# Early copies of two block products, later output products in batch 0, and weight combinations from four raw blocks

## The chip, the cores and the metric

One core of a Trainium2 chip runs the program. The metric is the time of one execution on the device, in microseconds (us); lower is better. The core has five engines with queues of their own: TensorE (PE; its weight loads are listed as PEld), VectorE (DVE), ScalarE (ACT), GpSimd (POOL), and SyncE (SP), whose queue issues the DMAs here.

## The reference

Three layers run one after the other over x of 4 batches, 1088 positions and 128 features, all in float32. The first is an attention with products of linear features, the second a gated channel mix, and the third, where the change lies, a gMLP block:

```python
h = np.maximum(x @ w_in, 0.0)                     # 128 -> 1024
u, v = h[..., :512], h[..., 512:]
v_n = (v - mu) / np.sqrt(var + 1e-06)             # over the 512 features
v_s = np.einsum('ts,bsd->btd', w_spatial, v_n) + b_spatial[None, :, None]
return ((u * v_s) @ w_out).astype(np.float32)     # 512 -> 128
```

w_spatial is 1088 x 1088: one matrix mixes the positions of every batch and feature.

## The kernel before

Matrices are held as a high part H (rounded to the matmul's 32-bit format) and a low part L = x - H. The helper `mm3` (line 124) multiplies such a pair by another in three matmuls. `copy` (line 127) makes H on ACT; `low` (line 130) makes L on DVE or POOL.

Attention and channel mix run up to about 206 us. The rest is the spatial product, in two ways.

**Batch 0** multiplies directly. A unit (function `spatial`) is one block d of 128 features by one chunk c of positions (384, 384 and 320 columns); `ORD0` lists the 12 units, four of which run earlier. A unit makes u (`pre` part, relu on ACT at line 519), sums eight position tiles k = 0..7 and a tail into `acc`, multiplies on DVE (line 529) and hands the result to `put_out`: H on ACT, L on DVE, and a closure in the list `gout`. A later unit pops that closure behind its own tile k == 3; it multiplies by w_out into a bank of PSUM. Between the tiles a unit also starts other work from the table `fill`: the tiles v of batch 1 (`v_tile`), and the combinations of weight blocks for the batches to come (`W2`).

**Batches 1 to 3** cut the positions 0..767 against 0..767 in blocks of two by two and use a scheme with seven block products in place of eight. It needs combinations of the four 384-wide raw blocks W11, W12, W21, W22 for each k of 0..3: part 1 = W12 - W11, part 3 = W22 - W12, part 2 = W22 - W12 + W11, part 4 = W21 - part 2. Part 4 takes the place of W12 in SBUF, which batch 0 reads for chunk 1. `first_load` and `first_sums` ("fl", "fs") read raw blocks by DMA (line 574) into slots of `VR`, make sums on DVE (`tt`, line 577) and split them (`parts`: ACT, then POOL). `second_load` and `second_sums` ("sl", "ss") do the rest. The slots 3 to 8 of `VR` serve these loads and later `quad_load` (line 632), which fetches blocks of the normalised v back from DRAM for `build`, which combines and splits them.

A **group** (function `group`) is one batch and a pair of feature blocks d, e = p, p + 2; there are six. Its products go to three banks: X (bank 0), Y (bank 1) and Z (bank 6). Each product (`prod`) is 12 matmuls; `tmm` (lines 675 and 676) adds the tail. Products 2 and 3 add to X, 4 adds to Z. `snap` copies a bank to SBUF on ACT, `join` adds a bank and such a copy on DVE (line 577), `gated_out` multiplies by relu of `pre` (line 689) and calls `put_out`. The end of a group before the change is

```python
prod(X, 3, 3, False); tmm(X, e, wtile(NK, 1))
u3 = snap(X)
gated_out(pre(e, 1), join(Z, u3, c22), e, 1)      # Z holds product 1
gated_out(pre(e, 0), join(Y, u3), e, 0)           # Y holds product 22 x 4
prod(Z, 4, 22, False)                             # adds to Z: after the join has read it
```

so the product 4 may not start before the join has read Z, and the next group's first product, which starts bank X afresh, not before `snap` has read X.

The program is written down as a list, and a planner, which uses a model of the engines' times, then orders the instructions of each engine: what it takes for ready goes ahead, earlier lines of the program first among ready ones. So a place in the program is a rank and no fixed slot; once planned, each engine runs its queue strictly in that order.

Of the kernel before, what the change touches and what calls it, by code (L numbers as in the profile page):

```python
# [19 lines left out]
DG = 512  # L20
# [41 lines left out]
W2 = {4: ((6, "fl", 2),), 5: ((1, "fs", 2), (1, "fl", 3)), 6: ((1, "fs", 3), (2, "fl", 0)),  # L62
      7: ((1, "fs", 0), (2, "fl", 1)), 8: ((1, "fs", 1), (4, "sl", 2), (4, "sl", 0)), 9: ((1, "ss", 2), (4, "ss", 0), (7, "sl", 1)),
      10: ((4, "ss", 1), (7, "sl", 3)), 11: ((4, "ss", 3),)}
FSET = ((3, 4, 5), (6, 7, 8))
SSET = {2: (7, 8), 0: (5, 6), 1: (7, 8), 3: (7, 8)}
# [12 lines left out]
def attn_moe_gmlp(ctx: ExitStack, tc: tile.TileContext, qT, kT, va, st, wk, wv, wr, win, wout,  # L79
# [325 lines left out]
    wt, xsp, vnt, tl, vdram = {}, {}, {}, {}, {}  # L405
# [50 lines left out]
    def v_tile(b, j, banks=(6, 7)):  # L456
        xH, xL = xsp[b]
        v = VR[:, j] if b == 0 else VR[:, rot(-1, -2, -3) + 3] if j < NK else vtail[:, 0]
        pv = bank(rot(*banks))
        cs = slice(128 * j, 128 * j + 128)  # L460
        mm3(pv, xH[:, cs], xL[:, cs], winH[:, DG:], winL[:, DG:], True, True, 0)
        SE.activation(out=v, in_=pv, func=AF.Relu)  # L462
        bn = sb(rot("bn0", "bn1"), [128, 6])
        mv = sb(rot("mv0", "mv1"), [128, 2])
        rs = sb(rot("rs0", "rs1"), [128, 1])
        VE.bn_stats(out=bn, in_=v)  # L466
        VE.bn_aggr(out=mv, in_=bn)
        GE.tensor_scalar(out=rs, in0=mv[:, 1:2], scalar1=1e-6, scalar2=None, op0=ALU.add)
        GE.tensor_tensor(out=rs, in0=rs, in1=half, op=ALU.pow)  # L469
        VE.tensor_scalar(out=v, in0=v, scalar1=mv[:, 0:1], scalar2=rs, op0=ALU.subtract, op1=ALU.mult)  # L470
        if b and j < NK:
            if j == 0:
                vdram[b] = dr.tile([128, NK, DG], F32, tag=f"vd{b}", bufs=1, name=f"vd{b}")
            nc.sync.dma_start(out=vdram[b][:, j], in_=v)
# [32 lines left out]
    def spatial(b, d, c, fill, early=False):  # L507
# [13 lines left out]
        for k in range(NK):  # L521
            mm3(acc, Hs[k], Ls[k], *wtile(k, c), k == 0, False, 0)
            if k == 3 and gout:
                gout.pop(0)()
            for fn in fill.get(k, ()):
                fn()
# [57 lines left out]
    def first_load(k):  # L584
        raws[k] = [stage(j) for j in rot(*FSET)]
        for x, n in zip(raws[k], (11, 12, 22)):
            wraw(x, n, k)
# [6 lines left out]
    def first_sums(k):  # L594
        r11, r12, r22 = raws.pop(k)
        tt(VE, r11, r12, r11, ALU.subtract)
        parts(1, k, r11)
        tt(VE, r22, r22, r12, ALU.subtract)
        parts(3, k, r22)

    def second_load(k):
        raws[k] = [stage(j) for j in SSET[k]]
        for x, n in zip(raws[k], (11, 21)):
            wraw(x, n, k)

    def second_sums(k):
        a, c = raws.pop(k)
        H, L = [x.bitcast(F32) for x in ctile(3, k)]
        tt(VE, a, a, H, ALU.add)
        tt(VE, a, a, L, ALU.add)  # L610
        tt(VE, c, c, a, ALU.subtract)
        parts(2, k, a)
        parts(4, k, c)
# [34 lines left out]
    def group(b, p):  # L648
# [50 lines left out]
        a = snap(X)  # L699
# [10 lines left out]
        gated_out(pu, join(Y, a), d, 0)  # L710
# [7 lines left out]
        tmm(Y, e, ctile(5, NK))  # L718
        flush()
# [12 lines left out]
        flush()  # L732
        yield
        Z = bank(6)[:, :CMAX]
        prod(Z, 1, 1, True)
        yield
        prod(X, 3, 3, False)
        tmm(X, e, wtile(NK, 1))
        u3 = snap(X)
        pu = pre(e, 1)  # L740
        c22 = sb(rot(m(8), m(9), m(10), m(11)), [128, CMAX])
        gated_out(pu, join(Z, u3, c22), e, 1)
        pu = pre(e, 0)
        gated_out(pu, join(Y, u3), e, 0)
        yield
        prod(Z, 4, 22, False)
        tmm(Z, d, wtile(NK, 1))
        if last_group:
            while gout:
                flush()  # L750
            pu = pre(d, 1)
# [207 lines left out]
    xsplit(1)  # L959
    for u, (d, c) in enumerate(ORD0):  # L960
        if u < EARLY:
            continue
        fill = {}

        def add(k, fn, *a):
            fill.setdefault(k, []).append(lambda: fn(*a))

        for k in range(WB[u] if u < len(WB) else 0):
            add(k, wstep)
        for n, j in enumerate({4: (0, 1), 5: (2, 3), 6: (4, 5), 7: (6, 7)}.get(u, ())):  # L970
            add(2 + 3 * n, v_tile, 1, j)
        for k, fn, *a in W2.get(u, ()):
            add(k, {"fl": first_load, "fs": first_sums, "sl": second_load, "ss": second_sums}[fn], *a)
        if u == 9:
            for n in (11, 12):
                add(2, quad_load, 1, 0, n)
        if u == 11:
            for n in (22, 21):
                add(0, quad_load, 1, 0, n)
        if u == 10:  # L980
            add(2, tails, 1, 0, vtail[:, 0])
            add(1, build, 1, 0, 0)
        if u == 11:
            add(1, build, 1, 0, 1)
        spatial(0, d, c, fill)
    assert wi[0] >= len(worder) and not pending_raw
    groups = [(b, p) for b in range(1, B) for p in range(2)]
    for gi, (b, p) in enumerate(groups):
        nxt = groups[gi + 1] if gi + 1 < len(groups) else None
        if gi == 0:  # L990
            tail_sums()
            build(1, 0, 2)
            tails(1, 2, vtail[:, 0])
            build(1, 0, 3)
        if p == 0 and b + 1 < B:
            xsplit(b + 1)
        for st, _ in enumerate(group(b, p)):
# [4 lines left out]
            if nxt:  # L1002
# [4 lines left out]
                if st in (5, 6):  # L1007
                    tails(nxt[0], nxt[1] + 2 * (st - 5), vtail[:, 0])
# [63 lines left out]
```

## Time and profile before

| | us |
|---|---|
| median of three runs | 472.14 (471.73 to 472.79) |
| profiled execution, whole | 474.71 |
| profiled execution, first to last instruction (span) | 472.9 |

The profile is of one execution. A stretch "206:271" counts from the start of the span. For PE the trace knows starts; a matmul's end is modelled, so in a dense row of matmuls each starts before the one ahead of it is shown as ended, and idle time is counted from the modelled end. PE is busy in 95% of the span, DVE in 61%, ACT in 55%, POOL in 52%.

### The profile page before, as it was taken

The numbers are of one execution on the slowest core, as the hardware profiler recorded it, in microseconds if no ns is written. First come the engines' busy times: TensorE is split into PE (matmuls) and PEld (weight loads), VectorE is DVE, ScalarE is ACT, GpSimd is POOL, SyncE is SP. The second block draws the span as 40 slices with busy tenths as digits, with TensorE's granted clock in tenths as the row PEclk, the third lists the DMA queues.
The fourth block names the chain that finished last, engine by engine and source line by source line (L and its number), as shares of the span: only waits on it lengthen the run. The fifth ranks groups of instructions, "written<-read, shape, count | busy, mean of one in ns | idle before, by whom it ended". The sixth has DMA issues, their size and how long they took to land.

```text
span 472.9 us, 7556 instructions
## 1 busy us (share of the span) xinstructions
PE 447.5 (95%) x2685; PEld 421.6 (89%) x2685; DVE 288.1 (61%) x501; ACT 260.6 (55%) x600; POOL 244.7 (52%) x287
## 2 busy tenths in 40 slices
PE   8978999999999998998988999999999999999995
PEld 8967998989998887998877999899899899999995
DVE  4598767767546795347785784772575751623513
ACT  2485878888776976784443644343535433433322
POOL 2566546486444988368645644445434534333320
PEclk9999999999999999999998999999999999999999
DMA  6973100011000120145454311313022222010001
GB/s 212 362 238 91 49 0 2 17 35 53 24 1 1 52 62 6 33 119 154 138 182 149 115 60 50 109 44 113 14 79 83 74 91 81 18 39 24 0 1 47
DMA packets 31525, 35.70 MB, mean 75 GB/s; under 512 B 2880, under 2 KB 27008, under 8 KB 31488
## 3 DMA queue, kind: packets, MB, share of 16 engines
q1 hardware_dynamic: 31488, 35.22, 23.3%
q8 instruction: 21, 0.34, 0.3%
q14 instruction: 16, 0.13, 0.1%
HBM read 26.69 MB, written 8.52 MB: 74 GB/s over the span
## 4 chain that ended last, share of the span: by engine, by line
PE 59%; DVE 16%; POOL 10%; DMA 5%; issue 4%; ACT 4%; SPq 1%; POOLq 0%; ACTq 0%; DVEq 0%
PE p L124 47%; DVE VR L470 4%; PE p L398 4%; DVE w L130 2%; DMA VR<-in_wT_dram 2%; POOL m L355 2%; PE p L270 2%; DVE bn L466 2%; POOL rs L469 2%; PE p L232 2%; DMA w<-in_wk_dram 2%; DVE w L140 1%; POOL w L130 1%; PE p L201 1%; DMA w<-in_qT_dram 1%
## 5 line engine op out<-in xcount | busy, mean ns | idle before, releaser
L124 PE MATMUL p<-m,k 128*128 128x384 f32 (+1 forms) x288 | 65.8, 348 | 2.7 <-POOL k L145 1.6
L124 PE MATMUL p<-w,k 128*128 128x384 f32 (+1 forms) x360 | 64.1, 324 | 2.4 <-DVE m L577 2.4
L355 POOL TENSOR_TENSOR m<-m 128x384 f32<-128x384 f32 (+1 forms) x48 | 42.8, 897 | 39.2 <-ACT m L352 33.6
L124 PEld LDWEIGHTS p<-w,k 128*128 128x128 f32 x360 | 59.1, 188 | 3.9 <-DVE m L577 3.3
L130 POOL TENSOR_TENSOR k<-VR,k 128x512 fp32r<-128x512 f32 x26 | 33.9, 1305 | 47.4 <-ACT k L127 35.4
L577 DVE TENSOR_TENSOR m<-p,m 128x384 f32<-128x384 f32 (+2 forms) x37 | 19.2, 520 | 61.0 <-PE p L676 34.1
L124 PEld LDWEIGHTS p<-m,k 128*128 128x128 f32 x288 | 48.3, 188 | 6.4 <-POOL k L145 1.8
L130 DVE TENSOR_TENSOR w<-m,w 128x384 fp32r<-128x384 f32 (+1 forms) x44 | 32.7, 751 | 28.5 <-POOL m L355 18.4
L352 ACT ACTIVATE m<-p 128x384 f32<-128x384 f32 (+1 forms) x96 | 42.4, 470 | 11.1 <-PE p L124 8.3
L127 ACT ACTIVATE m<-m 128x384 fp32r<-128x384 f32 (+2 forms) x45 | 22.7, 504 | 38.1 <-DVE m L689 27.0
L124 PE MATMUL p<-w,n1H 128*128 128x384 f32 (+1 forms) x192 | 39.1, 333 | 3.1 <-ACT m L127 2.9
L470 DVE TENSOR_SCALAR VR<-VR,mv,rs 128x512 f32<-128x512 f32 x33 | 31.6, 963 | 15.5 <-POOL rs L469 15.2
L130 DVE TENSOR_TENSOR m<-m,m 128x384 fp32r<-128x384 f32 (+1 forms) x47 | 29.9, 638 | 13.9 <-ACT m L127 8.8
L124 PEld LDWEIGHTS p<-w,n1H 128*128 128x128 f32 x192 | 32.9, 194 | 5.1 <-ACT m L127 4.3
L124 PE MATMUL p<-w,n1L 128*128 128x384 f32 (+1 forms) x168 | 37.4, 329 | 0.0
L127 ACT ACTIVATE k<-VR 128x512 fp32r<-128x512 f32 x26 | 16.2, 629 | 36.5 <-PE p L124 28.4
L398 PE MATMUL p<-w,wvT 128*128 128x384 f32 (+1 forms) x88 | 34.3, 471 | 0.0
L124 PEld LDWEIGHTS p<-w,n1L 128*128 128x128 f32 x168 | 29.2, 192 | 0.3
L466 DVE BATCH_NORM_STATS2 bn<-VR 128x6 f32<-128x512 f32 x33 | 22.5, 686 | 11.0 <-ACT VR L462 10.9
L124 PE MATMUL p<-m,woH 128*128 128x384 f32 (+1 forms) x86 | 26.6, 332 | 1.5 <-DVE m L130 1.5
L124 PE MATMUL p<-w,xs1H 128*128 128x384 f32 (+1 forms) x88 | 25.1, 339 | 2.9 <-DVE w L130 2.9
L130 POOL TENSOR_TENSOR n1H<-VR,n1H 128x512 fp32r<-128x512 f32 x12 | 15.5, 1292 | 23.1 <-ACT n1H L127 18.8
(263 smaller groups left out, 1163.9 us busy)
## 6 DMA issues: line engine op xcount, KB each, us to landing
vd<-VR SPq DMA_DIRECT2D x24, 256.0 KB, 2.0
VR<-vd SPq DMA_DIRECT2D x24, 256.0 KB, 2.9
VR<-in_wT_dram SPq DMA_DIRECT2D x20, 192.0 KB, 2.9
st<-in_wT_dram SPq DMA_DIRECT2D x16, 192.0 KB, 2.4
w<-in_kT_dram SPq DMA_DIRECT2D x8, 192.0 KB, 4.5
w<-in_qT_dram SPq DMA_DIRECT2D x8, 192.0 KB, 4.3
out_dram<-m SPq DMA_DIRECT2D x8, 192.0 KB, 1.9
st<-in_wT_dram SPq DMA_DIRECT2D x8, 160.0 KB, 2.4
```

Source lines behind the costliest of these rows:

```text
L124: TE.matmul(out_ap, lhsT=l, rhs=r, start=first and n == 0, stop=last and n == 2, skip_group_check=skip)
L127: return SE.activation(out=dst, in_=src, func=AF.Copy)
L130: return eng.tensor_tensor(out=L, in0=src, in1=H.bitcast(F32), op=ALU.subtract)
L232: TE.matmul(kv[:, w * g:w * g + w], lhsT=kp, rhs=vt if wide else vt[:, VP * g:VP * g + VP], start=(t == 0), stop=(t == NT - 1))
L270: nd_pe[0] = TE.matmul(o.rearrange("p h c -> p (h c)"), lhsT=qt[g][:, cut(c, t)], rhs=kb[:, g], start=not wide or g == 0, stop=not wide or ...
L352: SE.activation(out=r, in_=hk, func=AF.Relu)
L355: anchor[2] = GE.tensor_tensor(out=sq, in0=r, in1=r, op=ALU.mult)
L398: TE.matmul(vvs[i], lhsT=wvT[:, f // 2], rhs=hls.pop(g), start=f == 0, stop=f == NF - 1)
L466: VE.bn_stats(out=bn, in_=v)
L469: GE.tensor_tensor(out=rs, in0=rs, in1=half, op=ALU.pow)
L470: VE.tensor_scalar(out=v, in0=v, scalar1=mv[:, 0:1], scalar2=rs, op0=ALU.subtract, op1=ALU.mult)
L577: return eng.tensor_tensor(out=o, in0=a, in1=b_, op=op)
```

## The change

In a group, Y (product 22 x 4) and Z (product 1) are copied by `snap` as soon as they are done, as `m4` and `m5`; the copy `u3` is gone, and the two joins read X and these copies. The last group makes `pre(d, 1)` ahead of product 4. In batch 0 the closures of `gout` are popped behind tile 6. The first pass over the raw weights makes part 1 alone, from two loads; the second loads four blocks and makes parts 3, 2 and 4 with three sums. `v_tile` splits off its last step (the normalising multiplication, line 470, and the DMA to DRAM at line 474), which `v_rest` runs later, ahead of the next tile. The tiles of batch 1 move by a unit, the splitting of batch 1's x (`xsplit`) into the fifth unit, tails and quad loads to other places.

```diff
 ORD0 = ((0, 0), (1, 0), (0, 1), (1, 1), (2, 0), (3, 0), (2, 1), (3, 1), (0, 2), (1, 2), (2, 2), (3, 2))
-W2 = {4: ((6, "fl", 2),), 5: ((1, "fs", 2), (1, "fl", 3)), 6: ((1, "fs", 3), (2, "fl", 0)),
-      7: ((1, "fs", 0), (2, "fl", 1)), 8: ((1, "fs", 1), (4, "sl", 2), (4, "sl", 0)), 9: ((1, "ss", 2), (4, "ss", 0), (7, "sl", 1)),
-      10: ((4, "ss", 1), (7, "sl", 3)), 11: ((4, "ss", 3),)}
-FSET = ((3, 4, 5), (6, 7, 8))
-SSET = {2: (7, 8), 0: (5, 6), 1: (7, 8), 3: (7, 8)}
+W2 = {4: ((1, "fl", 0), (3, "fl", 1)), 5: ((3, "fs", 0), (4, "fl", 2), (6, "fs", 1), (7, "fl", 3)),
+      6: ((3, "fs", 2),), 7: ((1, "fs", 3), (2, "sl", 2)), 8: ((3, "ss", 2), (4, "sl", 0)),
+      9: ((1, "ss", 0), (6, "sl", 1)), 10: ((2, "ss", 1), (7, "sl", 3)), 11: ((3, "ss", 3),)}
+SSET = {2: (3, 4, 5, 6), 0: (7, 8, 5, 6), 1: (7, 8, 5, 6), 3: (7, 8, 5, 6)}
 R0 = (1, 5)
...
-    wt, xsp, vnt, tl, vdram = {}, {}, {}, {}, {}
+    wt, xsp, vnt, tl, vdram, vrest = {}, {}, {}, {}, {}, []
...
         GE.tensor_tensor(out=rs, in0=rs, in1=half, op=ALU.pow)
-        VE.tensor_scalar(out=v, in0=v, scalar1=mv[:, 0:1], scalar2=rs, op0=ALU.subtract, op1=ALU.mult)
-        if b and j < NK:
-            if j == 0:
-                vdram[b] = dr.tile([128, NK, DG], F32, tag=f"vd{b}", bufs=1, name=f"vd{b}")
-            nc.sync.dma_start(out=vdram[b][:, j], in_=v)
+
+        def rest():
+            VE.tensor_scalar(out=v, in0=v, scalar1=mv[:, 0:1], scalar2=rs, op0=ALU.subtract, op1=ALU.mult)
+            if b and j < NK:
+                if j == 0:
+                    vdram[b] = dr.tile([128, NK, DG], F32, tag=f"vd{b}", bufs=1, name=f"vd{b}")
+                nc.sync.dma_start(out=vdram[b][:, j], in_=v)
+
+        if b == 0:
+            rest()
+        else:
+            vrest.append(rest)
+
+    def v_rest():
+        while vrest:
+            vrest.pop(0)()
...
             mm3(acc, Hs[k], Ls[k], *wtile(k, c), k == 0, False, 0)
-            if k == 3 and gout:
+            if k == 6 and gout:
                 gout.pop(0)()
...
     def first_load(k):
-        raws[k] = [stage(j) for j in rot(*FSET)]
-        for x, n in zip(raws[k], (11, 12, 22)):
+        raws[1, k] = [stage(j) for j in rot((3, 4), (5, 6), (7, 8))]
+        for x, n in zip(raws[1, k], (11, 12)):
             wraw(x, n, k)
...
     def first_sums(k):
-        r11, r12, r22 = raws.pop(k)
+        r11, r12 = raws.pop((1, k))
         tt(VE, r11, r12, r11, ALU.subtract)
         parts(1, k, r11)
+
+    def second_load(k):
+        raws[2, k] = [stage(j) for j in SSET[k]]
+        for x, n in zip(raws[2, k], (12, 22, 11, 21)):
+            wraw(x, n, k)
+
+    def second_sums(k):
+        r12, r22, r11, r21 = raws.pop((2, k))
         tt(VE, r22, r22, r12, ALU.subtract)
         parts(3, k, r22)
-
-    def second_load(k):
-        raws[k] = [stage(j) for j in SSET[k]]
-        for x, n in zip(raws[k], (11, 21)):
-            wraw(x, n, k)
-
-    def second_sums(k):
-        a, c = raws.pop(k)
-        H, L = [x.bitcast(F32) for x in ctile(3, k)]
-        tt(VE, a, a, H, ALU.add)
-        tt(VE, a, a, L, ALU.add)
-        tt(VE, c, c, a, ALU.subtract)
-        parts(2, k, a)
-        parts(4, k, c)
+        tt(VE, r11, r22, r11, ALU.add)
+        parts(2, k, r11)
+        tt(VE, r21, r21, r11, ALU.subtract)
+        parts(4, k, r21)
...
         prod(X, 11, 11, True)
-        a = snap(X)
+        m1 = snap(X)
         flush()
...
         pu = pre(d, 0)
-        gated_out(pu, join(Y, a), d, 0)
+        gated_out(pu, join(Y, m1), d, 0)
         plain(acc, 12, False)
...
         tmm(Y, e, ctile(5, NK))
+        m4 = snap(Y)
         flush()
...
         u2 = snap(X)
-        flush()
         yield
...
         prod(Z, 1, 1, True)
+        m5 = snap(Z)
+        flush()
         yield
...
         tmm(X, e, wtile(NK, 1))
-        u3 = snap(X)
         pu = pre(e, 1)
-        c22 = sb(rot(m(8), m(9), m(10), m(11)), [128, CMAX])
-        gated_out(pu, join(Z, u3, c22), e, 1)
+        gated_out(pu, join(X, m5), e, 1)
         pu = pre(e, 0)
-        gated_out(pu, join(Y, u3), e, 0)
+        gated_out(pu, join(X, m4), e, 0)
         yield
+        if last_group:
+            pu = pre(d, 1)
         prod(Z, 4, 22, False)
...
                 flush()
-            pu = pre(d, 1)
             ob = sb(rot(m(6), m(7)), [128, CMAX])
...
     GE.tensor_copy(vtail[:, 0], VR[:, NK])
-    xsplit(1)
     for u, (d, c) in enumerate(ORD0):
...
             add(k, wstep)
-        for n, j in enumerate({4: (0, 1), 5: (2, 3), 6: (4, 5), 7: (6, 7)}.get(u, ())):
+        if u == EARLY:
+            add(0, xsplit, 1)
+        for n, j in enumerate({5: (0, 1), 6: (2, 3), 7: (4, 5), 8: (6, 7)}.get(u, ())):
+            add(2 + 3 * n, v_rest)
             add(2 + 3 * n, v_tile, 1, j)
...
         if u == 9:
+            add(2, v_rest)
             for n in (11, 12):
                 add(2, quad_load, 1, 0, n)
-        if u == 11:
-            for n in (22, 21):
-                add(0, quad_load, 1, 0, n)
         if u == 10:
             add(2, tails, 1, 0, vtail[:, 0])
-            add(1, build, 1, 0, 0)
+            add(4, build, 1, 0, 0)
         if u == 11:
             add(1, build, 1, 0, 1)
+            for n in (22, 21):
+                add(7, quad_load, 1, 0, n)
         spatial(0, d, c, fill)
...
         if gi == 0:
-            tail_sums()
             build(1, 0, 2)
...
             build(1, 0, 3)
+            tail_sums()
         if p == 0 and b + 1 < B:
...
                     quad_load(*nxt, (22, 21)[st - 3])
-                if st in (5, 6):
-                    tails(nxt[0], nxt[1] + 2 * (st - 5), vtail[:, 0])
+                if st in (3, 4):
+                    tails(nxt[0], nxt[1] + 2 * (st - 3), vtail[:, 0])
+            v_rest()
             if b + 1 < B:
```

## Rows read from the trace of the kernel before

**Rows 1.** By stretch: PE, PEld, DVE, ACT, POOL busy (x instructions), clock, DMA, GB/s.

```profile
206.00:271.40 65.40, 59.02 (x332) 55.69 (x331) 45.99 (x77) 34.06 (x79) 42.22 (x48) 0.97 0.48 148
...
304.50:337.60 33.10, 32.11 (x190) 31.39 (x191) 16.95 (x33) 13.77 (x30) 14.77 (x17) 1.00 0.22 69
```

**Rows 2.** PE in time at six group ends: start, us, what, idle before.

```profile
304.49 2.38 PE L124 MATMUL p<-w,k 128*128 128x384 f32 x12 [0.83 <-DVE m L577]
...
335.40 2.35 PE L124 MATMUL p<-w,n1H 128*128 128x384 f32 x12 [0.99 <-ACT m L127]
...
372.33 2.38 PE L124 MATMUL p<-w,k 128*128 128x384 f32 x12 [0.37 <-DVE m L577]
...
401.20 0.34 PE L676 MATMUL p<-w,wrH 128*128 128x384 f32 x1
402.66 2.35 PE L124 MATMUL p<-w,n1H 128*128 128x384 f32 x12 [1.12 <-ACT m L127]
404.85 2.26 PE L124 MATMUL p<-w,k 128*128 128x384 f32 x12
...
433.36 2.37 PE L124 MATMUL p<-w,n1H 128*128 128x384 f32 x12 [0.80 <-ACT m L127]
...
464.45 2.35 PE L124 MATMUL p<-w,k 128*128 128x384 f32 x12 [1.17 <-DVE m L577]
```

**Rows 3.** ACT and DVE in time, end of the last group.

```profile
463.31 0.49 ACT L127 ACTIVATE m<-p 128x384 f32<-128x384 f32 x1 [2.35 <-PE p L676]
...
463.83 0.56 DVE L577 TENSOR_TENSOR m<-p,m 128x384 f32<-128x384 f32 x1 [6.46 <-ACT m L127]
...
467.18 0.62 DVE L577 TENSOR_TENSOR m<-p,m 128x192 f32<-128x192 f32 x2
```

**Rows 4.** PE in time, late batch 0: each idle time from 206 on.

```profile
219.00 0.44 PE L124 MATMUL p<-xs0H,winL 128*128 128x384 f32 x1 [1.45 <-DVE x L402]
...
231.15 0.44 PE L124 MATMUL p<-m,woL 128*128 128x384 f32 x1 [0.87 <-ACT m L127]
...
232.56 0.45 PE L124 MATMUL p<-m,woH 128*128 128x384 f32 x1 [0.28 <-DVE m L130]
...
240.63 0.44 PE L124 MATMUL p<-m,woL 128*128 128x384 f32 x1 [2.03 <-ACT m L127]
...
253.72 0.41 PE L124 MATMUL p<-xs0H,winL 128*128 128x320 f32 x1 [0.54 <-ACT m L519]
...
256.39 0.67 PE L124 MATMUL p<-m,woH 128*128 128x384 f32 x1 [1.20 <-DVE m L130]
```

**Rows 5.** By stretch, just behind the last of these gaps; columns as before.

```profile
257.00:259.50 2.50, 2.50 (x11) 2.50 (x10) 0.49 (x1) 0.95 (x3) 1.00 (x2) 0.50 0.62 188
```

**Rows 6.** Form of the joins and sums (line 577): min/median/max ns.

```profile
L577 DVE TENSOR_TENSOR m<-p,m x37: 347/545/559, 279.7 to 467.5; 128x384 f32<-128x384 f32 x23, 128x320 f32<-128x320 f32 x12, 128x192 f32<-128x192 f32 x2
...
L577 DVE TENSOR_TENSOR VR<-VR,t x4: 542/900/1627, 235.8 to 264.3; 128x384 f32<-128x384 f32 x4
```

**Rows 7.** Waits from 271 us on: us in total, times, longest.

```profile
DVE VR L470 <- POOL rs L469: 10.8, 13, 1.0
```

**Rows 8.** DVE, then POOL, in time, late in batch 0.

```profile
238.18 1.31 DVE L577 TENSOR_TENSOR VR<-VR,x 128x384 f32<-128x384 f32 x1 [0.28 <-DMA VR<-in_wT_dram]
...
262.34 1.63 DVE L577 TENSOR_TENSOR VR<-VR,t 128x384 f32<-128x384 f32 x1 [4.57 <-DMA VR<-in_wT_dram]
...
262.26 1.29 POOL L130 TENSOR_TENSOR n1H<-VR,n1H 128x512 fp32r<-128x512 f32 x1 [4.18 <-issue]
```

**Rows 9.** Loads of raw weight blocks: count, size, median us to landing.

```profile
VR<-in_wT_dram SPq DMA_DIRECT2D x20, 192.0 KB, 2.9
```

**Rows 10.** POOL's low parts of the weight combinations (line 130): min/median/max ns.

```profile
L130 POOL TENSOR_TENSOR t<-VR,t x5: 1015/1018/1327, 216.9 to 227.5; 128x384 fp32r<-128x384 f32 x5
```

**Rows 11.** PE in time, first group: its start and third stage.

```profile
271.41 0.86 PE L124 MATMUL p<-w,n1H 128*128 128x384 f32 x4
...
283.45 2.26 PE L124 MATMUL p<-w,k 128*128 128x384 f32 x12
```

## The prediction

> **What bounds the kernel now.** I read the busy time by stretch first. From 206 us on, PE works nearly all the time: 59.0 of 65.4 us late in batch 0, 32.1 of 33.1 us in a group [rows 1]. No other engine is near that, and the change leaves the number of matmuls as it is, so only PE's idle time can be won or lost. Then I listed PE in order of time and looked at the brackets: the idle time in front of a matmul, and who ended it.
>
> In the groups there is one such place in each, always behind the last matmul of product 3: 0.83, 0.99, 0.37, 1.12, 0.80 and 1.17 us [rows 2]. The brackets are counted from a modelled end. In a dense row of 12 matmuls, shown as 2.26 us, the last is shown as 0.34, so each starts (2.26 - 0.34)/11 = 0.175 us behind the one before, and each bracket hides another 0.34 - 0.175 = 0.17 us [rows 2]. So the real stalls are 1.00, 1.16, 0.54, 1.29, 0.97 and 1.34: 6.3 us in all. The last one shows the whole chain: ACT copies X from 463.31 for 0.49, DVE joins at 463.83 for 0.56, product 4 starts at 464.45 [rows 2, 3]. In three groups the planner put the next group's first product there, and it waits for the same ACT copy; in two, product 4 waits for DVE, which is late.
>
> Late in batch 0 there are six idle places: 1.45, 0.87, 0.28, 2.03, 0.54 and 1.20 us [rows 4], 6.4 and with the hidden part 7.4. Behind the last one PE ran at a granted clock of 0.50, the lower level of 1.2 GHz, in 257.0 to 259.5 [rows 5]: half of 2.5 us, 1.25, is lost again. Batch 0 thus wastes 8.7 us, and the upper bound of any gain is 6.3 + 8.7 = 15.
>
> **The groups.** Removed: the copy u3 (0.49 on ACT), and the wait of product 4 for it and for the join. Added: two copies, one more on ACT than before, 6 x 0.49 = 2.9 us; ACT is busy 13.8 of 33.1 us [rows 1] and both copies are taken behind products whose banks are not needed for 12 matmuls (2.1 us), so they cost nothing unless ACT is held for over 1.5 us. Product 4 can then follow product 3 at once. What is late next is bank X: the next group's first product must wait until both joins have read it. From the end of product 3 that takes 0.2 us of start, then join, gate and join, some 0.56 each [rows 3, 6], 1.9 us; PE has product 4 and its tail, 14 matmuls or 2.45 us, to do meanwhile. The join keeps its form, one operand from PSUM and one from SBUF, 0.545 us at the median and 0.559 at most [rows 6]. In the groups with tiles of the next batch DVE also holds the tiles' chain: the last step of a tile waited for POOL 13 times, 10.8 us in all [rows 7], and everything behind it in DVE's queue waited along. Deferring it removes that, but I leave 0.3 us of stall for each of these two groups. The last group wins less: behind the joins DVE still has two gates and two low parts before the split join at 467.18 [rows 3], and only the copy's 0.5 us leaves this chain. Sum: 1.00 + 1.16 + 0.54 + 1.29 + 0.97 - 2 x 0.3 + 0.5 = 4.9 us. Bounds: 6.3 when nothing stays, and 3 when every group keeps a third of a microsecond or so more on bank X.
>
> **Batch 0.** The gap at 256.39 is an output product that waits for a low part made on DVE [rows 4]; its unit had begun at 253.72, only 2.7 us before, the wait included. Behind tile 6 come first the unit's own 3 + 7 x 3 = 24 matmuls of 320 columns, at 0.175 x 320/384 = 0.146 us each 3.5 us from its start, so the low part is there in time. With the gap goes the slow stretch: 1.37 + 1.25 = 2.6 us. The gap at 240.63 is another output product. The multiplication that makes its input stood behind a DVE sum that waited for a raw block until 238.18 and then took 1.31 [rows 4, 8]. The first pass now has two loads for each k in place of three and one sum in place of two, so I count this 2.2 us as gone. The remaining gaps, 1.62 + 1.04 + 0.45 + 0.71 = 3.8 us, I leave: I see no step that must remove them.
>
> Against this stands the second pass. It has four loads in place of two and three splits in place of two: 4 x 2 more loads late, 4 fewer early, and four splits (1.02 us each on POOL [rows 10]) moved from the first to the second. The number of sums there stays at three for each k, and in total falls from 20 to 16. Two of the four slots are the same for every k, so a load waits until POOL has read the slot, and DVE's sum waits for the load, 2.9 us [rows 9], with the unit's multiplication and low parts queued behind it. The same happened before at 262.34, where DVE stood 4.57 us and PE lost nothing [rows 8]. This cost no row of before shows; its bounds are nothing and one stall of 2.2 us as at 240.63 for each of the three handovers, 6.6. I take 2.0, near one stall, because output products now come later and so bear a late DVE better. Batch 0 sums to 2.6 + 2.2 - 2.0 = 2.8, bounds -1.8 (2.6 and 2.2, minus 6.6) and 8.7.
>
> One thing speaks against the move. A sum of two SBUF operands took between 0.542 and 1.627 us [rows 6], and the 1.63 one started 0.08 us after a POOL instruction that reads SBUF [rows 8]; the joins from PSUM never stretch. The Trainium skill (SBUF — State Buffer, section Who interferes with whom) says that DVE and GpSimd share one pair of ports as an exclusive lock, and that a DVE operation with two SBUF inputs blocks fully against a GpSimd operation that reads SBUF. By that rule, and the trace agrees, the four POOL splits that move into the second pass can each hold a sum or low part on DVE, and the total would be 468.7 us, as in the third rival; by the sum above, which lets DVE's free time take them, 464.4.
>
> The sum is 4.9 + 2.8 = 7.7 us. Made on the profiled execution it gives a span of 472.9 - 7.7 = 465.2 and 474.71 - 7.7 = 467.0 for the whole; that execution lies 2.6 us above the median of the runs, so for the runs I take 472.14 - 7.7 = 464.4 us.
>
> **The rivals.** (1) Batch 0 gives back what it wins and only the groups count: 472.14 - 4.9 = 467.2, or up to 469 with 3 from the groups. For it: all three handovers; against: later output products. (2) Nearly all stalls of batch 0 go as well, since fewer early loads also relieve the gaps at 231 and 219: 4.9 + 7 gives 460.2. (3) The four moved POOL splits stretch DVE by up to 1.627 - 0.542 = 1.09 us each, 4.3 in all, and DVE is what PE waits for in these units: 464.4 + 4.3 = 468.7. Against: DVE has 19.4 us free in 206 to 271.4 [rows 1]. (4) Slower: the second pass becomes a chain that ends too late. A cycle for one k is load 2.9, two sums of 0.56, an ACT copy 0.5 and two or three POOL splits of 1.02, with starts about 7 us. The unit that begins at 253.72 has one before it of 32 matmuls, 4.7 us, so chunk 1's blocks are free near 249 and the first split into them is done near 250.5. Three cycles lead to 271.5, a quad load (some 3, as a raw block's) and a build (some 2) to 276.5. PE wants the parts 4 and that build in the group's third stage, at 283.45, 12 us from its start at 271.41 [rows 11]; with batch 0's last three gaps gone, near 280. So 4 us are free. It eats the whole 7.7 us once a cycle takes over 7 + (4 + 7.7)/3 = 10.9 us; at 12 it costs 3 x 5 - 4 = 11 and the time is 475.4. (5) The change does not do what it says: the planner orders the group end so that PE meets a wait of an equal length on bank X, and batch 0 nets nothing: 472 give or take 0.9.
>
> **How the numbers follow.** Chances: forecast 0.52, (1) 0.17, (3) 0.08, (2) 0.10, (4) 0.08, (5) 0.05. The forecast's own range is 461 to 467.5. The range of 8 in 10 leaves out (4), (5), the upper part of (1) and half of (2): 459.8 to 469.5. A difference of 0.2%, 0.9 us, is about what a measurement of this kernel can tell from no change. Faster: 0.52 + 0.17 + 0.08 + 0.10 = 0.87; same 0.05; slower 0.08.
>
> **What the profile after would show.** Right: behind product 3 the 12 matmuls of product 4 follow without idle time in five of six groups; joins that read X twice; no idle time where PE starts the next group; no wait of line 470 for POOL in the groups; no idle time near 256 and no stretch at clock 0.50. Wrong: idle time in front of the next group's first product, released by DVE line 577; DVE idle for raw blocks with PE idle behind it in the last four units; PE idle in the first group's third stage for POOL or a part 4; a slow stretch of the clock elsewhere.

## The result, and the profile after

The changed kernel took 468.12 us at the median (466.96 to 468.68, four executions) against 471.99 for the kernel before: a ratio of 0.9912 with a 95% interval of 0.9889 to 0.9935, 3.9 us less. Measured again it took 467.36 against 472.06, ratio 0.9895 (0.9876 to 0.9914). So it is faster, and 468.12 lies in the forecast's range of 459.8 to 469.5, but 3.7 us above the forecast of 464.4. The profiled execution took 466.96 us with a span of 465.2, which is just the span forecast; that agreement is partly luck, as will be seen, since the profiled execution of before lay 2.6 us above its median and this one 1.2 us below. That the time lies in the range is partly luck as well: the two parts of the forecast were wrong in opposite directions, and the errors partly cancel.

The same two stretches as in [rows 1], PE, PEld, DVE, ACT, POOL busy, clock, DMA share and GB/s, and 2.5 us at the end of batch 0, in the changed kernel:

```profile
206.00:271.40 65.40, 61.03 (x344) 55.93 (x342) 43.41 (x72) 32.66 (x76) 38.84 (x47) 1.00 0.50 152
304.50:337.60 33.10, 33.10 (x199) 32.71 (x198) 18.20 (x34) 14.84 (x34) 16.54 (x19) 1.00 0.19 62
272.00:274.50 2.50, 2.50 (x11) 2.50 (x10) 1.65 (x3) 1.96 (x6) 1.28 (x2) 0.50 0.51 150
```

In this stretch of the groups PE now has no idle time at all: 33.10 of 33.10 us, where it had 32.11 [rows 1]. In batch 0 it is busy for 2.0 us more up to 271.4, but the stretch at clock 0.50, which stood behind 256.39 [rows 5], is there again, at 272.

PE in time, at the second and the last of the six places of [rows 2]: the last row of product 3's tail, then product 4, and in the second group the next group's first product behind it.

```profile
332.24 0.34 PE L684 MATMUL p<-w,wrH 128*128 128x384 f32 x1
332.42 2.26 PE L123 MATMUL p<-w,k 128*128 128x384 f32 x12
...
334.88 2.27 PE L123 MATMUL p<-w,n1L 128*128 128x384 f32 x12
...
456.50 0.34 PE L684 MATMUL p<-w,wrH 128*128 128x384 f32 x1
456.68 2.26 PE L123 MATMUL p<-w,k 128*128 128x384 f32 x12
```

Here and at the other four places no row has a bracket, and the next matmul starts some 0.18 us behind the last one of the tail, the step of a dense row. All six stalls are gone, the last group's too. DVE at the end of the last group, answering to [rows 3]:

```profile
456.95 1.02 DVE L587 TENSOR_TENSOR m<-p,m 128x384 f32<-128x384 f32 x2 [6.00 <-PE p L684]
...
459.56 0.61 DVE L587 TENSOR_TENSOR m<-p,m 128x192 f32<-128x192 f32 x2
460.10 0.55 DVE L129 TENSOR_TENSOR m<-m,m 128x384 fp32r<-128x384 f32 x1
```

In the last group both joins run directly behind product 3, and the split join stands ahead of the second low part, which I had put in front of it.

PE in time late in batch 0, its idle times from 249 us on (two more, of 0.33 and 0.74 us, stand at 227 and 235), with the group's first matmul and the start of its third stage, answering to [rows 4, 11]:

```profile
249.56 0.44 PE L123 MATMUL p<-m,woL 128*128 128x384 f32 x1 [0.38 <-ACT m L126]
...
255.98 0.41 PE L123 MATMUL p<-m,woL 128*128 128x320 f32 x1 [0.25 <-ACT m L126]
...
261.30 0.41 PE L123 MATMUL p<-xs0H,winL 128*128 128x320 f32 x1 [0.32 <-ACT m L529]
...
263.30 0.41 PE L123 MATMUL p<-m,woH 128*128 128x320 f32 x1 [0.70 <-DVE m L129]
...
266.93 0.69 PE L123 MATMUL p<-w,n1H 128*128 128x384 f32 x3
...
271.64 0.47 PE L123 MATMUL p<-m,woH 128*128 128x320 f32 x1 [1.86 <-DVE m L129]
...
282.54 1.73 PE L123 MATMUL p<-w,k 128*128 128x384 f32 x9
```

The first group starts 4.5 us earlier than in [rows 11], but its third stage only 0.9 us earlier: between the two lies the rest of batch 0, with a new idle time of 1.86 us and the slow stretch behind it. What DVE did ahead of it, and POOL beside it:

```profile
266.31 0.56 DVE L587 TENSOR_TENSOR VR<-VR 128x384 f32<-128x384 f32 x1 [2.67 <-DMA VR<-in_wT_dram]
...
268.35 0.70 DVE L587 TENSOR_TENSOR m<-m,m 128x384 f32<-128x384 f32 x1 [1.01 <-DMA m<-in_btail_dram]
268.97 0.95 DVE L129 TENSOR_TENSOR xs0L<-x,xs0H 128x384 fp32r<-128x384 f32 x2
269.84 1.34 DVE L587 TENSOR_TENSOR VR<-VR 128x384 f32<-128x384 f32 x1
271.11 0.48 DVE L129 TENSOR_TENSOR m<-m,m 128x320 fp32r<-128x320 f32 x1
```

```profile
269.69 1.08 POOL L129 TENSOR_TENSOR m<-m,m 128x384 fp32r<-128x384 f32 x1 [1.05 <-ACT m L126]
```

PE waits for the low part at 271.11. Ahead of it in DVE's queue a sum waited 2.67 us for a raw block, another 1.01 us for the load of `tail_sums`, and the last sum took 1.34 us instead of 0.56, beside a POOL instruction of 1.08 us that also reads SBUF. This is the queue that the prediction priced at 2.0 us, and the question is what it and the rest of batch 0 really cost.

### The profile page after: what moved, and what is told of

Read it like the earlier page. It is cut to its first block, busy times and chain, and to the rows that moved or that the text cites. A ratio compares the mean times of both kernels' runs of the same rounds, so it can differ in the third digit from the quotient of the medians.

```text
span 465.2 us, 7573 instructions
## 1 busy us (share of the span) xinstructions
PE 446.7 (96%) x2685; PEld 421.0 (90%) x2685; DVE 288.1 (62%) x497; ACT 264.9 (57%) x606; POOL 243.5 (52%) x287
## 4 chain that ended last, share of the span: by engine, by line
PE 64%; DVE 11%; POOL 9%; DMA 8%; issue 3%; ACT 3%; SPq 1%; POOLq 0%; DVEq 0%; ACTq 0%
PE p L123 49%; DMA VR<-in_wT_dram 4%; PE p L397 3%; PE p L231 3%; DVE w L129 3%; PE p L269 3%; PE p L200 2%; POOL m L354 2%; DVE VR L587 1%; DVE VR L471 1%; PE p L684 1%; PE p L683 1%; PE p L252 1%; POOL w L129 1%; DMA w<-in_qT_dram 1%
## 5 line engine op out<-in xcount | busy, mean ns | idle before, releaser
L129 POOL TENSOR_TENSOR k<-VR,k 128x512 fp32r<-128x512 f32 x26 | 35.1, 1351 | 31.7 <-ACT k L126 28.9
L129 DVE TENSOR_TENSOR m<-m,m 128x384 fp32r<-128x384 f32 (+1 forms) x47 | 33.5, 713 | 16.3 <-ACT m L126 11.0
L471 DVE TENSOR_SCALAR VR<-VR,mv,rs 128x512 f32<-128x512 f32 x33 | 34.1, 1039 | 12.5 <-POOL rs L468 12.2
L123 PE MATMUL p<-w,n1H 128*128 128x384 f32 (+1 forms) x192 | 41.2, 333 | 0.2 <-DVE x L539 0.2
L126 ACT ACTIVATE m<-p 128x384 f32<-128x384 f32 (+2 forms) x39 | 18.3, 471 | 32.7 <-PE p L123 23.4
L587 DVE TENSOR_TENSOR VR<-VR 128x512 f32<-128x512 f32 (+1 forms) x40 | 28.6, 714 | 13.2 <-DMA VR<-in_wT_dram 9.4
L123 PE MATMUL p<-w,n1L 128*128 128x384 f32 (+1 forms) x168 | 34.3, 325 | 0.0
```

What stands on the lines that cost most here:

```text
L123: TE.matmul(out_ap, lhsT=l, rhs=r, start=first and n == 0, stop=last and n == 2, skip_group_check=skip)
L126: return SE.activation(out=dst, in_=src, func=AF.Copy)
L129: return eng.tensor_tensor(out=L, in0=src, in1=H.bitcast(F32), op=ALU.subtract)
L587: return eng.tensor_tensor(out=o, in0=a, in1=b_, op=op)
```

## The experiments

**Both kernels again.**

> The kernel before, unchanged, profiled once more. Two theories of why the profiles differ by 7.7 us and the medians by 3.9. Theory S (the profiled execution of before was a long one): the span is near 470 us in place of 472.9, the six group stalls are the same, some 6.3 us, and batch 0 loses less than 8.7 us, some 6, with no stretch at half clock or a shorter one. Theory R (the profile of before is typical, and the profile after is a short one): the span is again near 472.9, with the same six gaps of 7.4 us and the slow stretch in batch 0.

> The changed kernel, unchanged, for a narrower interval and a second profile. Both theories: 0.3% around 468.1 us, ratio 0.9905 to 0.993. Under theory S the batch-0 part of the profile changes little; under theory R the span is 1 to 2 us above 465.2 and the extra lies in batch 0 (before the first group's third stage).

The changed kernel took 467.36 us (466.02 to 468.07), before 472.06. Its second profile has a span of 466.3 us, and the first group's third stage starts at 283.63 in place of 282.54, so that the whole 1.1 us lies ahead of it. The new profile of before, a single execution of 473.38 us with a span of 471.6, between the two theories' figures, shows the six group ends with the same brackets (0.86, 0.99, 0.37, 1.12, 0.80, 1.17), and late in batch 0 two of its idle times are:

```profile
239.28 0.44 PE L124 MATMUL p<-m,woL 128*128 128x384 f32 x1 [0.58 <-ACT m L127]
...
255.16 0.69 PE L124 MATMUL p<-m,woH 128*128 128x384 f32 x1 [1.22 <-DVE m L130]
```

The 2.03 us at 240.63 [rows 4] vary from one execution to another: here the same place has 0.58, and in the profile of the groups alone (below) 2.05. The idle time near 256 is steady.

**The groups alone, and all but the groups.** One kernel takes the new group into the kernel before, the other puts the old group into the changed kernel:

```diff
         tmm(Y, e, ctile(5, NK))
+        m4 = snap(Y)
...
         prod(Z, 1, 1, True)
+        m5 = snap(Z)
...
-        u3 = snap(X)
...
-        gated_out(pu, join(Z, u3, c22), e, 1)
+        gated_out(pu, join(X, m5), e, 1)
...
-        gated_out(pu, join(Y, u3), e, 0)
+        gated_out(pu, join(X, m4), e, 0)
```

> Before with the change to the groups alone (early copies m4 and m5, joins that read X, the last group's early pre). Theory G (the groups give all of their 6.3 us, and batch 0 gives about 2.5 back): 465.6 us. Theory H (the groups give 3.9 and batch 0 nets nothing): 468.1 us. My prediction's own terms (4.9 from the groups): 467.1 us. In all of them no idle time behind product 3 in five or six groups.

> After with the old group function: batch 0's changes, the weight combinations and the deferred last step of a tile alone. Theory G: slower than before by about 2.5 us, 474.5. Theory H: as before, 472. My prediction's own terms (batch 0 wins 2.8): 469.2 us.

The groups alone took 465.55 us (465.38 to 467.26), ratio 0.9873 (0.9853 to 0.9893): 6.5 us less between the medians, 5.1 to 6.9 by the interval. From 275 us on its trace has no idle time on PE. All but the groups took 474.0 us (473.62 to 476.01), ratio 1.0051 (1.0033 to 1.0069): 1.9 us more than before, 1.6 to 3.3 by the interval. Both times are close to theory G's. The trace of all but the groups still shows the old group ends:

```profile
303.85 2.38 PE L123 MATMUL p<-w,k 128*128 128x384 f32 x12 [1.68 <-DVE m L587]
...
463.77 2.35 PE L123 MATMUL p<-w,k 128*128 128x384 f32 x12 [1.17 <-DVE m L587]
```

So the two halves have opposite signs, and the medians add up: -6.5 + 1.9 = -4.6, against the -4.7 measured for both in the same comparison. The whole gain is the groups', and the rest takes back some 2 us. By the medians the changed kernel is beaten by half of itself, though the two intervals still overlap.

Two things blur these figures. All four executions of the groups alone had a mean granted clock of 0.995; before had one so low in only 5 of 42, and against the median of these five, 472.81, the groups are worth 7.3 us. And a part of the 1.9 us is no cost of batch 0: the first group's end waits 1.68 us where it waited 0.83 [rows 2]. The traces separate the two parts better. Product 3 of the first group ends with this tail in before, and with the groups alone:

```profile
299.96 0.33 PE L675 MATMUL p<-w,T 128*128 128x384 f32 x1
```

```profile
299.40 0.33 PE L675 MATMUL p<-w,T 128*128 128x384 f32 x1
```

From there to the end of the span are 472.9 - 299.96 = 172.9 us in before, the same in its second profile, and 465.5 - 299.40 = 166.1 with the groups alone; the same sum gives 165.9 in the changed kernel and 173.5 in all but the groups. So the groups are worth 6.8 us, or 7.0 in the changed kernel. Ahead of this point the loss is between 1.9 - 0.6 = 1.3 us (all but the groups) and 7.0 - 4.7 = 2.3 us (the changed kernel), an estimate from a profile and medians.

**Only Z copied early.** In the group-only kernel `m4` is left out, and `u3` is kept for the join with Y:

```diff
-        m4 = snap(Y)
...
+        u3 = snap(X)
...
-        gated_out(pu, join(X, m4), e, 0)
+        gated_out(pu, join(Y, u3), e, 0)
```

> Before with the early copy of Z (product 1) alone: u3 is still copied from X on ACT, the first join adds two copies in SBUF, the second reads Y as before. If the group's gain is that product 4 no longer waits for the join to read Z: the same time as the whole change of the groups, 465.6 us, and no idle time behind product 3. If instead it is the joins' reading of X, or bank Y's earlier release, that wins: 468 us or more, with the next group's first product or product 4 waiting behind product 3.

It took 466.86 us (465.98 to 467.57) against 472.04, ratio 0.9892 (0.9876 to 0.9908), between the two figures expected, and two idle times remain in the groups:

```profile
301.64 2.35 PE L124 MATMUL p<-w,n1H 128*128 128x384 f32 x12 [0.55 <-DVE m L577]
...
367.70 2.35 PE L124 MATMUL p<-w,n1H 128*128 128x384 f32 x12 [0.21 <-DVE m L577]
```

The early copy of Z brings 5.2 of the 6.5 us; from the tail of the first group's product 3 to the end, as above, it is 464.8 - 297.10 = 167.7 us, 5.2 of the 6.8. The two brackets, with 0.17 us hidden in each, make 1.1 us, about the 1.3 us that are missing to the full group change; the intervals of the two kernels touch, so this second part rests on the rows more than on the times.

**The closures behind tile 6, alone.** On top of the new groups:

```diff
-            if k == 3 and gout:
+            if k == 6 and gout:
```

> The groups' change and the pop of the output closures behind tile 6, nothing else of batch 0. Theory K: 467.5 us. Theories W and D, and the prediction's own step (the gap at 256 and its slow stretch go, 2.6 us): 463 to 465.5 us; by the prediction no idle time near 256 and no clock of 0.50 behind it.

It took 465.98 us (465.61 to 467.67), ratio 0.9887 (0.9868 to 0.9907): no gain over 465.55, and neither figure expected. PE, DVE and POOL in time around the place of 256.39:

```profile
253.37 0.41 PE L124 MATMUL p<-xs0H,winL 128*128 128x320 f32 x1 [0.51 <-ACT m L519]
...
253.78 0.44 PE L124 MATMUL p<-m,woL 128*128 128x384 f32 x1
...
256.05 0.44 PE L124 MATMUL p<-m,woH 128*128 128x384 f32 x1 [1.21 <-DVE m L130]
```

```profile
253.50 1.23 DVE L470 TENSOR_SCALAR VR<-VR,mv,rs 128x512 f32<-128x512 f32 x1 [0.53 <-POOL rs L469]
254.65 1.35 DVE L130 TENSOR_TENSOR m<-m,m 128x384 fp32r<-128x384 f32 x1
```

```profile
253.43 1.02 POOL L130 TENSOR_TENSOR w<-VR,w 128x384 fp32r<-128x384 f32 x1
254.40 1.18 POOL L130 TENSOR_TENSOR n0H<-VR,n0H 128x384 fp32r<-128x384 f32 x1
```

The gap stands where it stood. The output product begins 0.4 us after its unit, and not behind 24 matmuls. It did so in before too, where the closure is popped behind tile 3 and the unit begins at 253.72 [rows 4]:

```profile
254.13 0.45 PE L124 MATMUL p<-m,woL 128*128 128x384 f32 x1
```

So the planner starts its first matmuls as soon as the high part is there, whatever line they come from, and the third then waits in PE's strict order for the low part. That low part took 1.35 us here, where the same shape takes 0.55 to 0.56 at other places of these traces, and the tile step ahead of it 1.23 in place of 0.55, both beside POOL's splits: together 1.5 us, which covers the 1.38 us of the stall. No run takes POOL's splits away, so this cause is read from the rows and not tested. The Trainium skill (SBUF — State Buffer, section Who interferes with whom) has DVE's second input come through ports that it shares with GpSimd; the low part, which reads two SBUF operands, agrees.

**The new weight combinations alone, and with other slots.** On top of the new groups: the tables `W2` and `SSET`, the loads and sums of both passes and the quad loads behind the last sum. 

```diff
-        for x, n in zip(raws[k], (11, 12, 22)):
+        for x, n in zip(raws[1, k], (11, 12)):
...
-        for x, n in zip(raws[k], (11, 21)):
+        for x, n in zip(raws[2, k], (12, 22, 11, 21)):
...
-        tt(VE, a, a, H, ALU.add)
-        tt(VE, a, a, L, ALU.add)
-        tt(VE, c, c, a, ALU.subtract)
+        tt(VE, r11, r22, r11, ALU.add)
...
+        tt(VE, r21, r21, r11, ALU.subtract)
```

The second kernel changes one line more:

```diff
-SSET = {2: (3, 4, 5, 6), 0: (7, 8, 5, 6), 1: (7, 8, 5, 6), 3: (7, 8, 5, 6)}
+SSET = {2: (3, 4, 5, 6), 0: (7, 8, 3, 4), 1: (5, 6, 7, 8), 3: (5, 6, 7, 8)}
```

> The groups' change and the new weight combinations (four raw loads in the second pass, three splits), nothing else of batch 0. The groups alone ran in 465.55 us, all of the change in 467.4 to 468.1, so some 2 us are given back. Theory W (the second pass costs them, the 2.0 us that the prediction charged): 467.5 us, PE idle in the last four units behind DVE sums that wait for raw blocks. Theory K (the later output products cost them) and theory D (the deferred or moved tiles of batch 1 cost them): 465.5 us.

> The groups' change and the new weight combinations, as in the run of 469.2 us, with one edit: the second pass takes its slots in another rotation, so that a block's load waits for readers that are a step further back. If the hand-over of slots sets the loss of 3.6 us: 466.5 us or less, DVE's waits for raw blocks (12.7 us from 206 on) cut by half. If it is the load itself (more loads, and more POOL splits beside DVE's work late in batch 0): 468.5 to 469.5 us.

The combinations took 469.19 us (468.66 to 470.4), ratio 0.995 (0.9933 to 0.9967), 3.6 us more than the groups alone. DVE in time, then ACT, then PE, then DVE's waits for raw blocks between 206 and 275 us (us in total, times, longest):

```profile
260.46 1.15 DVE L576 TENSOR_TENSOR VR<-VR 128x384 f32<-128x384 f32 x2 [4.82 <-DMA VR<-in_wT_dram]
```

```profile
261.06 0.52 ACT L126 ACTIVATE n0L<-VR 128x384 fp32r<-128x384 f32 x1 [5.24 <-DVE VR L576]
...
263.90 0.44 ACT L518 ACTIVATE m<-p 128x320 f32<-128x320 f32 x1
```

```profile
264.39 0.41 PE L123 MATMUL p<-xs0H,winL 128*128 128x320 f32 x1 [1.61 <-ACT m L518]
...
276.97 0.42 PE L123 MATMUL p<-m,woL 128*128 128x320 f32 x1 [1.47 <-ACT m L126]
```

```profile
DVE VR L576 <- DMA VR<-in_wT_dram: 12.7, 9, 4.8
```

A sum waited 4.82 us for its load, and ACT 5.24 us for the sum. The relu (line 518 here) that PE waits for at 264.39 stands in ACT's queue behind the copies that begin at 261.06, so PE meets the late load by way of ACT. With the other slots the kernel took 466.25 us (465.94 to 467.19), ratio 0.9884 (0.9868 to 0.9899), and its waits were

```profile
DVE VR L576 <- DMA VR<-in_wT_dram: 8.9, 6, 4.3
```

The same loads and sums, 2.9 us less by other slots alone: that much of the 3.6 us is the hand-over of slots, the cost that the prediction could take from no row. The waits fell by 3.8 us and not by half, and the 0.7 us left for the number of loads, sums and splits is within the noise. The prediction took the hand-over for smaller than it is: it counted two slots that are the same for every k, but in the order of the loads (k = 2, 0, 1, 3) all four are the same from the second k on.

**The tiles a unit later, alone.** On top of the new groups, only the moves of batch 1's tiles, of `xsplit` and of `build`:

```diff
-    xsplit(1)
...
-        for n, j in enumerate({4: (0, 1), 5: (2, 3), 6: (4, 5), 7: (6, 7)}.get(u, ())):
+        if u == EARLY:
+            add(0, xsplit, 1)
+        for n, j in enumerate({5: (0, 1), 6: (2, 3), 7: (4, 5), 8: (6, 7)}.get(u, ())):
...
-            add(1, build, 1, 0, 0)
+            add(4, build, 1, 0, 0)
```

> The groups' change and the tiles of batch 1 a unit later, with the split of its x inside the fifth unit, nothing else of batch 0. Theory D: 467 us or so. Theories W and K: 465.5 us or a little less, the gap at 219 (a wait for a DVE multiplication queued behind the split of x) gone, some 1 us.

It took 467.65 us (467.31 to 468.23), ratio 0.9916 (0.99 to 0.9933): 2.1 us more than the groups alone, for a step that the prediction did not price. DVE, POOL and PE in time:

```profile
268.79 0.56 DVE L577 TENSOR_TENSOR m<-m,m 128x384 f32<-128x384 f32 x1 [4.93 <-DMA m<-in_btail_dram]
...
270.13 4.12 DVE L130 TENSOR_TENSOR xs0L<-x,xs0H 128x384 fp32r<-128x384 f32 x3
...
274.66 0.49 DVE L529 TENSOR_TENSOR m<-p,m 128x320 f32<-128x320 f32 x1
```

```profile
271.06 3.11 POOL L130 TENSOR_TENSOR k<-VR,k 128x512 fp32r<-128x512 f32 x2
```

```profile
276.07 0.42 PE L124 MATMUL p<-m,woL 128*128 128x320 f32 x1 [1.30 <-ACT m L127]
```

DVE stands for 4.93 us at the load of `tail_sums`; three low parts behind it (1.7 us at 0.55 each) run at the same time as POOL's splits and take 4.12 us; the last unit's multiplication comes behind them, and PE waits 1.30 us for what follows from it. But the groups alone have nearly the same chain on DVE, and no idle time on PE from 256 us on:

```profile
269.44 3.03 DVE L130 TENSOR_TENSOR xs0L<-x,xs0H 128x384 fp32r<-128x384 f32 x3
...
273.88 0.49 DVE L529 TENSOR_TENSOR m<-p,m 128x320 f32<-128x320 f32 x1
```

The difference is that PE begins the last unit's long row of matmuls at 263.76 here and at 266.88 there: it comes earlier to a chain that ends 0.8 us later. How the 2.1 us are made up is not shown by this. The gap at 219, which two of the theories expected gone, is still 1.52 us.

**The deferred tile step, alone.** On top of the new groups, `v_tile` with its last step split off, and the calls of `v_rest`:

```diff
+        def rest():
+            VE.tensor_scalar(out=v, in0=v, scalar1=mv[:, 0:1], scalar2=rs, op0=ALU.subtract, op1=ALU.mult)
...
+            add(2 + 3 * n, v_rest)
             add(2 + 3 * n, v_tile, 1, j)
...
+            v_rest()
```

> The groups' change and the deferred last step of a tile (line 470 and its DMA run later), nothing else of batch 0. Theory D: 467 us or so. Theories W and K: 465.5 us, since without the old joins no group waits on DVE any more and the 10.8 us of waiting for POOL lie beside PE's work.

It took 464.94 us (464.1 to 466.1), ratio 0.986 (0.9839 to 0.9881), the best median of all, 0.6 us below the groups alone; the intervals overlap, so this gain is not shown. Waits of the tile step for POOL from 271 us on, in this kernel:

```profile
DVE VR L472 <- POOL rs L469: 7.1, 9, 1.0
```

The groups alone show the same total, 7.1 us in 9 waits, and before had 10.8 in 13 [rows 7]: the fall comes with the new groups, and the deferral adds nothing to it in this stretch.

**All but the new combinations.** The changed kernel with the old tables, loads and sums, and with two quad loads in their old place:

```diff
-W2 = {4: ((1, "fl", 0), (3, "fl", 1)), 5: ((3, "fs", 0), (4, "fl", 2), (6, "fs", 1), (7, "fl", 3)),
...
+W2 = {4: ((6, "fl", 2),), 5: ((1, "fs", 2), (1, "fl", 3)), 6: ((1, "fs", 3), (2, "fl", 0)),
...
```

> All of the change except the weight combinations, which are the old ones (five loads and five sums for each k). If the combinations are what costs in batch 0: 464.5 to 465.5 us, below both the changed kernel (467.4 to 468.1) and the groups alone (465.55). If the tiles a unit later cost by themselves, as their single run says (467.65): 466.5 to 467.5 us.

It took 467.96 us (466.77 to 469.05), ratio 0.9909 (0.9894 to 0.9925), no less than the changed kernel's 467.36 and 468.12, and a little above the second figure expected. On top of the later tiles the new combinations cost nothing that shows, though alone they cost 3.6 us. DVE's longest wait is again the load of `tail_sums`, 5.3 us.

**The changed kernel with the other slots.** The full change, with the line `SSET` altered as above:

```diff
-SSET = {2: (3, 4, 5, 6), 0: (7, 8, 5, 6), ...
+SSET = {2: (3, 4, 5, 6), 0: (7, 8, 3, 4), 1: (5, 6, 7, 8), ...
```

> The changed kernel with one line altered: the four slots of the second pass are (3, 4, 5, 6), (7, 8, 3, 4), (5, 6, 7, 8), (5, 6, 7, 8) for k = 2, 0, 1, 3, so that the loads of the third k do not wait for two slots that the second k still holds. Theory 1, the loss of the full change late in batch 0 comes from the hand-over of slots, as it does where the new combinations stand alone (469.2 to 466.3): the time falls by 2 us or more, to 465.4 or less, and DVE's waits for raw blocks, 9.4 us between 206 and 275 us in the changed kernel, shrink to about 6. Theory 2, in the full change the tiles of batch 1, a unit later, bind instead (without the new combinations the same kernel still took 468.0): 467 to 468.2, with PE idle by over 1 us late in batch 0 behind DVE.

It took 466.6 us (466.11 to 468.34) against 471.58 for before on that chip, ratio 0.9895 (0.9873 to 0.9917). DVE's waits for raw blocks, here and in the changed kernel:

```profile
DVE VR L587 <- DMA VR<-in_wT_dram: 4.0, 6, 1.3
```

```profile
DVE VR L587 <- DMA VR<-in_wT_dram: 9.4, 8, 2.7
```

The waits shrink as the first theory said, and the idle time of 1.86 us at the end of batch 0 becomes 0.56. But others of 1.21, 0.99 and 0.89 us, at 236, 252 and 258 us, stand ahead of it, and the time doesn't follow: 0.8 us below the changed kernel's second median and 1.5 below its first, with a ratio equal to the second one's. Neither theory's figure was met; the result lies between them, and by the interval it is not told apart from the changed kernel.

## Why the prediction was right, and where it was off

**What bounds the kernel** held: PE's idle time is all that moved, and every gain or loss followed above shows as idle time of PE or as a slow stretch.

**The groups** went the way described, with the term mis-sized: 4.9 forecast, 6.5 measured (6.8 by the traces). All of the six real stalls, 6.3 us by the rows with the hidden 0.17 us in each, could be won, the upper bound; where the rest of the 6.8 lies was not followed. The 0.3 us left for each group with tiles did not occur. In the last group 1.3 us were won, from product 3's tail to the end (472.9 - 462.93 before, 465.2 - 456.50 after); the limit of 0.5 us fell as the planner put the split join ahead of the second low part. The copies cost nothing, as said. The early copy of Z is the larger part of it, as it lets product 4 follow at once.

**Batch 0** is the step that failed: a gain of 2.8 us forecast, a loss of 1.9 measured (1.3 to 2.3 with the traces), at the far end of the bounds (a loss of 1.8). The forecast stayed in its range because the groups won 1.6 us more than their term and so covered a third of this error. Its terms, one by one:

- The 2.6 us at 256.39. The step "behind tile 6 come first the unit's own 24 matmuls" is wrong: the trace with that edit alone shows the output product 0.4 us into its unit, and the gap unchanged; the trace of before had shown the same place. I had myself written that a place in the program is a rank and no slot, and then counted it as a slot. And the 1.25 us in it for the slow clock were hardly there to win: of 42 timed executions of before, 5 had a mean granted clock of 0.995 (median 472.81 us), the other 37 of 0.998 to 1.0 (471.76). Both profiled ones were of the rare kind, and I took the 1.25 off a median that doesn't hold it. In the full change the gap did go (0.25 us are left at 255.98), by which of its parts was not settled, but 1.86 us arose at 271.64, and there 6 of 9 executions have a clock of 0.996 (median 467.95), the other 3 of 0.998 to 1.0 (466.65).
- The 2.2 us at 240.63. They are not steady: another profile of before has 0.58 there, that of the groups alone 2.05.
- The 2.0 us for the second pass's slots. That loads wait for slots and DVE's sums for the loads was right, and alone it costs 2.9 us, within the bound of 6.6. Where the trace of the combinations alone shows PE waiting for it, the way is through ACT's queue.
- The tiles a unit later, 2.1 us alone, were not costed at all. With them PE comes earlier to the last units and waits there for DVE, which stood 4.93 us at the load of `tail_sums`.

The two last costs don't add: with both, and the rest, batch 0 loses some 2 us and not 5. Which part of the full change takes back the difference was not settled; nor was why the changed kernel with other slots still lies about 1 us above the groups alone.

**The rivals.** The first, that only the groups count, is close in its figure (467.2, with 468.12 and 467.36 measured) and in one reason, the three hand-overs, but batch 0 gave back more than it won, and larger groups covered that. The third, 468.7, is as close to the first measurement, but not in its reason. POOL stretching DVE is seen in single places (1.34 us at 269.84, 4.12 in the kernel with later tiles), but the sums were not stretched more than before: 0.558 us at the median of 16 in the changed kernel. The fourth did not come: PE is not idle in the first group's third stage. The fifth failed with the groups.

**The signs named beforehand.** Met: product 4 without idle time behind product 3, joins that read X twice, no idle time at the next group's start, none to speak of near 256. Not met: the tile step's waits for POOL remain with 6.8 us in 9, while PE has no idle time in the groups. Of the signs against, two came: DVE idle for raw blocks with PE idle behind it, and the slow stretch elsewhere.

## What to carry to other kernels

Copying an accumulator bank out as soon as it is complete, so that the late join reads the copy, was worth the whole of the stalls that it removed here; their sum, with the part hidden by modelled ends, gave 6.3 us where 6.5 were measured and the traces show 6.8. The new groups with the deferred tile step (464.94 us) beat both kernels here, so halves of a change are worth timing apart. Where a planner orders the queues, a moved line is only a changed rank: look in a trace for where the instruction would be ready, and try, for loads that feed an engine's queue, the slots that were read longest ago: it won 2.9 us where the combinations stood alone, and nothing that shows in the full change.

## What the runs showed of the hardware that was not expected

The same idle time is not always followed by the slow clock. A gap of 1.20 to 1.22 us near 255 us is in both profiles of before and in those of the groups alone, of the closures alone and of the deferred step alone. The granted clock in 250 to 260 us, a mean, is 0.83 in both profiles of before and with the groups alone, and 1.00 with the closures alone and with the deferred step; the second profile of before and that of the deferred step:

```profile
250.00:260.00 10.00, 8.38 (x44) 7.74 (x43) 4.88 (x8) 3.88 (x10) 4.97 (x6) 0.83 0.54 164
```

```profile
250.00:260.00 10.00, 8.22 (x53) 7.58 (x52) 4.48 (x7) 5.51 (x14) 6.02 (x7) 1.00 0.46 142
```

How often it falls differs by kernel: 5 of 42 timed executions of before, 6 of 9 of the changed kernel, 4 of 4 of the groups alone, none of 6 of the changed kernel with the other slots (mean clocks of 0.996 or less). Between the medians of before's executions with and without it lie 1.05 us. The Trainium skill (TensorE: Matmul & The Clock Gate, section What's actually happening) says that the chip's check of activity runs free and does not start anew with a kernel, which would let one program meet it differently from run to run; no run here varies that by itself.
